# A planned one-core attention and feed-forward kernel: products take tiles by their own gates, GpSimd does three of the clears, and the order table is made anew

## The chip, the cores and the metric

The kernel runs on one core of one Trainium2 chip. The metric is the device time in microseconds (us) of one execution. Engines are named as in the profile: PE is TensorE, which multiplies; PEld is its weight load; DVE is VectorE, ACT is ScalarE, POOL is GpSimd and SP is SyncE. POOL, SP and ACT also issue DMA transfers.

## The reference

There are 8 batches of 8 heads, 576 positions and 64 values a head. Attention adds a bias that depends on the distance of two positions and on the head; its output is laid out as 4608 tokens of 512 values and goes through a feed-forward layer of 2048 with a periodic gate.

```python
scores = q @ k.T / 8 + bias_table[bucket(|i - j|)]      # 32 buckets, one value a head
attn   = exp(scores) / sum(exp(scores))
x      = (attn @ v) laid out as 4608 x 512
h      = x @ w_in                                        # 4608 x 2048
s      = sin(alpha * h)
g      = h + s * s / alpha
out    = g @ w_out                                       # 4608 x 512, float32
```

## The kernel before

**Attention.** A batch is called t, a pair of heads p. K and Q are needed with the head's 64 values on the partitions. For the first two batches (and Q of the third) POOL loads natural tiles into xT, and PE turns them by transposes (L1089; the very first pair in halves, L1069, out of two loads that SP and ACT issue and that DVE and ACT cast, L931 and L933). For later batches POOL stages 16-bit copies in device memory (L990), and SP's queue loads them turned (L996). Scores are products of 64 rows at a time (L1148), with the last 64 positions apart (L1109, L1114, L1138). ACT takes the exponential of 1024 columns at once into a tile u (L1155); DVE multiplies the part near the diagonal by the exponential of the bias (L1176, L1160, L1163). PE multiplies by V (L1190, L1199), DVE divides (L1209, L1210), and the result is turned into xT, by PE for batch 0 (L1223) and by SP's queue after that (L1216).

**Feed-forward.** The tokens go in nine blocks of 480 to 576. For each block there are 16 units, one for each 128 of the 2048 columns. In a unit PE makes four products of 512 columns (L1242), ACT takes the sine (L1249), DVE squares it (L1253) and makes the gate g (L1267), which also sets the unit's accumulator free. An output tile is 128 tokens; it needs 16 products with w_out (L1276), one for each unit's gate, which the kernel emits as eight pieces of two. DVE then copies the tile out (L1282) and SP stores it (L1285). Accumulators lie in eight banks; units use banks 0 to 5, and a score tile takes a pair of banks.

**Order.** `_graph` makes a list of tasks with an engine, a cost and the tasks that each depends on, and `_Plan.run` plays them through in time: each engine takes the next task as soon as its dependencies, its buffers and its banks allow. If the table LINE is given, each engine takes its tasks in that table's order (a text of differences between task numbers), and the play-through settles what remains: how the engines' streams interleave in the program and which bank each product gets. The engines then execute in exactly that order; a task that waits holds up all that stands behind it on its engine.

**Where the change touches.** In `moe_out` a tile's first piece waits for all 16 gates of its blocks (`deps += G_done[b]`), each tile waits for the last piece of the tile before it (`state["mo"]`), and `held` keeps a first unit of the next block ahead of the fourth tile. `memsets` (L951 to L960, DVE) clears five kinds of tile before the first casts. POOL's first transfer (L963) stands first in its queue. The planner's cost of `memsets`, of the first loads and of POOL's first transfer stand in `_graph`.

Of the kernel before, what the change touches and what calls it, by code (L numbers as in the profile page):

```python
# [406 lines left out]
def _graph(K, opt):  # L407
    plan = _Plan()
# [4 lines left out]
    add = plan.add  # L413
# [16 lines left out]
    for half in range(2):  # L430
        for kind in range(2):
            first[kind][half] = add("ACT" if kind else "SP", 0.45, E("first_load", kind, half),
                                    lat=3.6 - 0.4 * kind if half else 2.95, prio=-9 + 0.3 * half)
# [4 lines left out]
    t_ms = add("DVE", 2.4, E("memsets"), prio=-10)  # L438
# [11 lines left out]
    def gq(dur, f, args, deps=(), pipe=1.0, pkt=58):  # L450
        return add("POOL", dur, E(f, *args), deps=deps, pipe=pipe, seq="GQ", pkt=pkt)

    def load_nat(t, p):
        for kind in range(2):
            if (t, p) != (0, 0) and (t < 2 or kind in nat2):
                T_nat[t][p][kind] = gq(0.67 if plan.nseq.get("GQ") else 1.3, "load_nat",
                                       (t, p, kind), pipe=0.78, pkt=90)
# [257 lines left out]
    BLK = _blocks(opt["blk"])  # L715
# [40 lines left out]
    def moe_out(tau):  # L756
# [4 lines left out]
        early = bs[-1] == len(BLK) - 1 and opt["early_mo"]  # L761
        np_ = opt["mo_n"]
        fn = NF // np_
        for piece in range(np_):
            fs = range(fn * piece, fn * piece + fn)
            deps = [T_wout[fs[-1] // 4]]
            for b in bs:
                deps += [G_done[b][f] for f in fs]
                if not piece and not early:
                    deps += G_done[b]  # L770
            if last is not None:
                deps.append(last)
            elif tau:
                deps.append(state["mo"])
            m = add("PE", 0.2158 * fn, None, deps=deps, prio=opt["p_mo"] - 0.01 * (piece > 0),
                    take=[(1, users)] if piece == 0 else [], mode="full", name=f"mo{tau}")
            if piece == 0:
                j = tau - state["tau0"]
                if bs[-1] + 1 < NBLK - 1 and j in opt["hold"]:
                    held.setdefault((bs[-1] + 1, opt["hold"][j]), []).append(m)  # L780
                m.emit = lambda m=m, fs=fs: K.moe_out(cell, tag(m), tau, fs)
            else:
                m.emit = lambda fs=fs: K.moe_out(cell, None, tau, fs)
            last = m
# [49 lines left out]
    0}, early_mo=False, mo_n=8, ins={-1: {16: 16}, 0: {}, 1: {5: 16}, 2: {15: 16}, 7: {15: 12,  # L834
# [8 lines left out]
class _Ops:  # L843
# [105 lines left out]
    def memsets(self):  # L949
        nc = self.nc  # L950
        nc.vector.memset(self.blank, 0.0)  # L951
        for i in range(2):
# [6 lines left out]
            nc.vector.memset(self.kd[i], 0.0)  # L959
            nc.vector.memset(self.us[i], 0.0)  # L960
# [377 lines left out]
```

## Time and profile before

| | us |
|---|---|
| median of three runs | 391.63 |
| lowest and highest | 390.82, 392.54 |
| the profiled execution | 391.27 |
| its span, first to last instruction | 389.4 |

The span is 1.87 us shorter than the profiled execution's time. In the rows quoted below, a line of the timeline has the start, the length, the engine, the source line, the operation, what it writes and reads, the shape and the count of instructions; in brackets stands the idle time of the engine before it and what ended that. Matmul lengths include a tail in the pipeline, so a group of back-to-back matmuls ends later than the next one starts. The table of stages gives for each engine the busy us in a stretch, then the clock that TensorE was granted as a share of full speed.

### The profile page before, as it was taken

The numbers are of one execution on the slowest core, as the hardware profiler recorded it, in microseconds if no ns is written. First come the engines' busy times: TensorE is split into PE (matmuls) and PEld (weight loads), VectorE is DVE, ScalarE is ACT, GpSimd is POOL, SyncE is SP. The second block draws the span as 40 slices with busy tenths as digits, with TensorE's granted clock in tenths as the row PEclk, the third lists the DMA queues.
The fourth block names the chain that finished last, engine by engine and source line by source line (L and its number), as shares of the span: only waits on it lengthen the run. The fifth ranks groups of instructions, "written<-read, shape, count | busy, mean of one in ns | idle before, by whom it ended". The sixth has DMA issues, their size and how long they took to land.

```text
span 389.4 us, 9321 instructions
## 1 busy us (share of the span) xinstructions
PE 372.6 (96%) x3811; PEld 202.0 (52%) x3811; DVE 297.2 (76%) x738; ACT 279.6 (72%) x339; POOL 85.8 (22%) x101
## 2 busy tenths in 40 slices
PE   2989979999999999999999999999999999999996
PEld 1567435665446545564555545544654445444442
DVE  5588897769967798759966986799649879978422
ACT  2799878899799868996799689958986874343100
POOL 7685734081006200900090004000000000000000
PEclk9999998999999999999999999999999999999999
DMA  9999999999739994999299839600420020201014
GB/s 162 184 186 187 195 182 145 158 116 184 85 77 138 138 61 106 109 179 150 39 153 150 117 64 171 89 14 0 117 62 0 29 72 28 72 0 56 0 56 162
DMA packets 148170, 40.79 MB, mean 105 GB/s; under 512 B 134416, under 2 KB 143456, under 8 KB 148128
## 3 DMA queue, kind: packets, MB, share of 16 engines
q0 software_dynamic: 96656, 18.45, 62.3%
q1 hardware_dynamic: 50768, 21.22, 26.6%
q8 instruction: 30, 0.49, 0.5%
q10 hardware_dynamic: 704, 0.53, 0.5%
q14 instruction: 12, 0.10, 0.1%
HBM read 36.94 MB, written 15.93 MB: 136 GB/s over the span
## 4 chain that ended last, share of the span: by engine, by line
PE 85%; DMA 11%; POOL 2%; DVE 1%; issue 0%; ACTq 0%; ACT 0%; SPq 0%; POOLq 0%
PE acc L1276 33%; PE acc L1242 28%; PE acc L1199 9%; PE acc L1148 8%; DMA xT<-in_q_dram 4%; DMA w_in<-in_moe_w_in_dram 2%; PE acc L1190 2%; PE acc L1109 2%; DMA v<-in_v_dram 2%; DMA cst_sb<-cst 2%; PE acc L1138 1%; DMA toep<-e_sb 1%; POOL xT L963 1%; PE acc L1089 0%; POOL mt L1042 0%
## 5 line engine op out<-in xcount | busy, mean ns | idle before, releaser
L1155 ACT ACTIVATE u<-acc 128x1024 f16<-128x1024 f32 x160 | 154.6, 1026 | 19.4 <-PE acc L1148 15.3
L1276 PE MATMUL acc<-w_out,g 128*128 128x512 f16 x576 | 145.9, 381 | 0.0
L1249 ACT ACTIVATE s<-acc,alphaT 128x512 f16<-128x512 f32 (+2 forms) x144 | 96.1, 688 | 58.0 <-PE acc L1242 32.5
L1242 PE MATMUL acc<-xT,w_in 128*128 128x512 f16 (+2 forms) x640 | 134.9, 358 | 0.0
L1267 DVE SCALAR_TENSOR_TENSOR g<-s,inv_a,acc 128x512 f16<-128x512 f16 (+4 forms) x176 | 107.5, 646 | 1.5
L1242 PEld LDWEIGHTS <-w_in 128*128 128x128 f16 x640 | 59.0, 98 | 67.0 <-issue 0.7
L1276 PEld LDWEIGHTS <-g 128*128 128x128 f16 x576 | 50.8, 98 | 53.9 <-issue 8.1
L1253 DVE TENSOR_TENSOR s<-s 128x512 f16<-128x512 f16 (+2 forms) x144 | 57.2, 420 | 16.8 <-ACT s L1249 16.5
L1176 DVE TENSOR_TENSOR u<-u,toep 128x1024 f16<-128x1024 f16 (+1 forms) x128 | 58.9, 486 | 14.3 <-ACT u L1155 13.8
L969 POOL DMA_DIRECT2D v<-in_v_dram x32 | 28.3, 897 | 144.8 <-PE acc L1199 136.5
L1199 PE MATMUL acc<-v,u 128*128 128x65 f16 x1280 | 53.9, 193 | 0.0
L1199 PEld LDWEIGHTS <-u 128*128 128x128 f16 x1280 | 49.9, 97 | 4.2
L1148 PE MATMUL acc<-qT,kT 64*128 64x256 f16 x512 | 45.0, 282 | 3.6 <-DVE g L1267 1.9
L1282 DVE COPY outs<-acc 128x512 f32<-128x512 f32 x36 | 24.6, 688 | 20.4 <-PE acc L1276 18.8
L1148 PEld LDWEIGHTS <-kT 64*128 64x128 f16 x512 | 19.5, 96 | 26.7 <-issue 23.6
L1210 DVE TENSOR_TENSOR xp<-acc,rden 128x256 f16<-128x256 f32 (+1 forms) x64 | 31.4, 491 | 2.2
L1190 PE MATMUL acc<-vt,u 128*128 128x130 f16 x128 | 28.3, 221 | 0.3 <-DMA vt<-in_v_dram 0.3
L1209 DVE RECIPROCAL rden<-acc 128x4 f32<-128x4 f32 (+1 forms) x64 | 11.9, 185 | 20.3 <-PE acc L1199 20.2
L1190 PEld LDWEIGHTS <-u 128*128 128x128 f16 x128 | 12.4, 97 | 8.0 <-issue 2.9
L990 POOL DMA_DIRECT2D staged_q<-in_q_dram x5 | 13.9, 2780 | 0.0
L990 POOL DMA_DIRECT2D staged_k<-in_k_dram x6 | 13.5, 2257 | 0.9 <-DMA xT<-in_q_dram 0.9
L1249 ACT ACT_TABLE_LOAD x9 | 11.5, 1283 | 0.2
(62 smaller groups left out, 163.6 us busy)
## 6 DMA issues: line engine op xcount, KB each, us to landing
out_dram<-outs SPq DMA_DIRECT2D x36, 256.0 KB, 2.4
v<-in_v_dram POOLq DMA_DIRECT2D x32, 128.0 KB, 7.3
staged_k<-in_k_dram POOLq DMA_DIRECT2D x6, 576.0 KB, 13.0
staged_q<-in_q_dram POOLq DMA_DIRECT2D x5, 576.0 KB, 15.4
w_in<-in_moe_w_in_dram POOLq DMA_DIRECT2D x4, 512.0 KB, 8.6
w_out<-in_moe_w_out_dram POOLq DMA_DIRECT2D x4, 512.0 KB, 10.1
xT<-in_q_dram POOLq DMA_DIRECT2D x11, 144.0 KB, 7.8
xT<-in_k_dram POOLq DMA_DIRECT2D x7, 144.0 KB, 6.9
```

Of the source, the lines that this page charges most:

```text
L969: self.nc.gpsimd.dma_start(out=self.vs[t % 2][:, c, :, 0:D], in_=src)
L1148: self.nc.tensor.matmul(out=s[:, o:o + 256], lhsT=self.kT[t % 2][r, p, 128 * c:128 * c + 128], rhs=self.qT[t % 2][r, p, 256 * w:256 * w + ...
L1155: self.nc.scalar.activation(out=c["u"], in_=c["s"], func=AF.Exp, scale=0.125)
L1176: self.nc.vector.tensor_tensor(out=io, in0=io, in1=m, op=ALU.mult)
L1190: nc.tensor.matmul(out=c["av"][:, 130 * j:130 * j + 130], lhsT=tail, rhs=vt[:, p, :], start=True, stop=True, skip_group_check=True)
L1199: nc.tensor.matmul(out=c["av"][:, 130 * j + 65 * a:130 * j + 65 * a + 65], lhsT=l, rhs=vv[:, ch, 2 * p + a, 0:65], start=False, stop=True, ...
L1210: self.nc.vector.tensor_tensor(out=self.ap(x, 256 * w, [[64, n], [1, 64]]), in0=self.ap(av, 0, [[65, n], [1, 64]]), in1=self.ap(r, 0, [[1, ...
L1242: self.nc.tensor.matmul(out=c["h"][:, x:y], lhsT=self.w_in[:, j, 128 * f:128 * f + 128], rhs=self.xT[:, j, lo + x:lo + y], start=(j == 0), ...
L1249: self.nc.scalar.activation(out=c["s"], in_=c["h"], func=AF.Sin, scale=self.alphaT[:, f:f + 1])
L1253: self.nc.vector.tensor_tensor(out=c["s"], in0=c["s"], in1=c["s"], op=ALU.mult)
L1267: self.nc.vector.scalar_tensor_tensor(out=o, in0=c["s"][:, x:y], scalar=self.inv_a[:, f:f + 1], in1=c["h"][:, x:y], op0=ALU.mult, op1=ALU.add)
L1276: self.nc.tensor.matmul(out=c["mo"], lhsT=self.g[b][:, f, 128 * (tau % 4):128 * (tau % 4) + 128], rhs=self.w_out[:, f, :], start=(f == 0), ...
```

## The change

1. `moe_out`: the option `early_mo` is gone, and a new option `strict`, which is False, switches off three things: the first piece's wait for all gates of its blocks, the wait for the tile before, and the hold against the next block's first unit. A piece now depends on its own two gates, its weights and the piece before it in its own tile.
2. Clears: `blank`, the two `kd` and the two `us` tiles are no longer cleared by DVE. A new task `clear` has POOL do it, ahead of POOL's first transfer. Per partition these are 2 x 320, 2 x 512 and 256 values of 16 bits, 1920 in all, in five instructions.
3. Costs in `_graph`: 1.5 for the DVE clears (2.4 before), 1.0 for the new ones, 0.9 for the first transfer of POOL (1.3 before), and changed latencies of the first loads.
4. LINE is replaced by another table, so that the order on every engine is another.

```diff
-                                    lat=3.6 - 0.4 * kind if half else 2.95, prio=-9 + 0.3 * half)
+                                    lat=3.4 - 0.1 * kind if half else 2.95 - 0.25 * kind, prio=-9 + 0.3 * half)
...
-    t_ms = add("DVE", 2.4, E("memsets"), prio=-10)
+    t_ms = add("DVE", 1.5, E("memsets"), prio=-10)
+    add("POOL", 1.0, E("clear"), seq="GQ")
...
-                T_nat[t][p][kind] = gq(0.67 if plan.nseq.get("GQ") else 1.3, "load_nat",
+                T_nat[t][p][kind] = gq(0.67 if plan.nseq.get("GQ") > 1 else 0.9, "load_nat",
...
-        early = bs[-1] == len(BLK) - 1 and opt["early_mo"]
...
-                if not piece and not early:
+                if not piece and opt["strict"]:
                     deps += G_done[b]
             if last is not None:
                 deps.append(last)
-            elif tau:
+            elif tau and opt["strict"]:
                 deps.append(state["mo"])
...
-                if bs[-1] + 1 < NBLK - 1 and j in opt["hold"]:
+                if opt["strict"] and bs[-1] + 1 < NBLK - 1 and j in opt["hold"]:
...
     def memsets(self):
         nc = self.nc
-        nc.vector.memset(self.blank, 0.0)
         for i in range(2):
...
-            nc.vector.memset(self.kd[i], 0.0)
-            nc.vector.memset(self.us[i], 0.0)
+
+    def clear(self):
+        nc = self.nc
+        for i in range(2):
+            nc.gpsimd.memset(self.us[i], 0.0)
+            nc.gpsimd.memset(self.kd[i], 0.0)
+        nc.gpsimd.memset(self.blank, 0.0)
```

What the new table does to the order on PE around block 0, in names of the tasks (a piece is two products with w_out; "1 of tile 0" is its first piece):

```text
before: units 0.0 0.1, V product, units 0.2 to 0.15, turns of (2,1) and (2,0), score a, score b,
        turn, two scores, turn, score, pieces 1 2 of tile 0, scores, piece 3 of tile 0, ...
after:  units 0.0 0.1, V product, units 0.2 to 0.6, piece 1 of tile 1, unit 0.7, piece 1 of tile 0,
        units 0.8 to 0.12, piece 2 of tile 0, unit 0.13, piece 2 of tile 1, units 0.14 0.15,
        piece 3 of tile 1, score a, piece 4 of tile 1, piece 3 of tile 0, piece 5 of tile 1,
        pieces 4 5 of tile 0, two scores, piece 6 of tile 1, turn of (2,3), score b,
        pieces 7 8 of tile 1, scores, piece 6 of tile 0, V product of (1,0), ...
```

At the start, PE's order was: half turns of K and Q, with a whole turn of pair 1 second in the queue, the bias and the other halves between, then the first scores. Now it is three half turns (K, Q, K), the bias product, the first scores, the last half turn, and only then the turns of pair 1. DVE casts both halves of K before Q's.

More of the change, by code (lines that the diff above doesn't have):

```diff
@@ L833 @@
     line=_line(LINE), c_act=((1, 1),), h_act=(), p_bias=-0.5, nu=12, ng=3, first=(1, 1, 1), bs=2, win=7, hold={3:
-    0}, early_mo=False, mo_n=8, ins={-1: {16: 16}, 0: {}, 1: {5: 16}, 2: {15: 16}, 7: {15: 12,
+    0}, strict=False, mo_n=8, ins={-1: {16: 16}, 0: {}, 1: {5: 16}, 2: {15: 16}, 7: {15: 12,
     16: 4}, 5: {17: 16}, 4: {18: 16}}, s_at={0: 9, 1: 9}, blk=(512, 512, 512, 512, 512, 512,
```

100 rows, old and new, of the table LINE are left out of this document.

## The prediction

> **What bounds the kernel now.** First the page's busy times and slices, then the stages, then PE's waits.
>
> ```profile
> span 389.4 us, 9321 instructions
> PE 372.6 (96%) x3811; PEld 202.0 (52%) x3811; DVE 297.2 (76%) x738; ACT 279.6 (72%) x339; POOL 85.8 (22%) x101
> PE   2989979999999999999999999999999999999996
> ...
> DVE  5588897769967798759966986799649879978422
> ```
>
> PE is busy for 372.6 of 389.4 us and hardly stops between slice 7 and the end. The products are the same ones after the change, so a gain can only come from the 16.8 us in which PE stands idle, from stretches where it runs slowly, or from less switching of its array. The stages say where these are:
>
> ```profile
> core 0: us, PE busy (x) PEld busy (x) DVE busy (x) ACT busy (x) POOL busy (x), PEclk, DMA share, GB/s
> 0.00:22.00 22.00, 13.18 (x191) 9.00 (x191) 12.72 (x39) 11.80 (x15) 16.41 (x31) 1.00 1.23 174
> 22.00:39.40 17.40, 16.08 (x376) 12.71 (x368) 14.66 (x45) 16.66 (x21) 12.38 (x19) 1.00 1.47 185
> 39.40:55.00 15.60, 14.90 (x86) 6.69 (x82) 14.49 (x33) 12.58 (x18) 8.76 (x11) 1.00 1.56 193
> 55.00:63.50 8.50, 6.28 (x93) 3.25 (x93) 7.65 (x16) 7.08 (x10) 6.21 (x5) 0.80 1.67 150
> 63.50:90.00 26.50, 26.50 (x427) 17.15 (x426) 17.86 (x56) 23.57 (x26) 9.52 (x9) 1.00 1.70 141
> 130.00:389.00 259.00, 255.67 (x2236) 131.80 (x2232) 196.91 (x473) 173.44 (x213) 23.25 (x22) 1.00 0.66 80
> ```
>
> Up to 39.4 us lies the set-up with batch 0; from 22 us on ACT leads there (16.66 of 17.40). Then come block 0's units. The stage from 55 to 63.5 is the odd one: PE idles for 2.2 us and its granted clock is 0.80, the only one below 1.00. After that PE is full; 3.3 us idle remain in the last 259, most of them the final copy and store. What happens at 55 us:
>
> ```profile
> 54.49 0.69 ACT L1249 ACTIVATE s<-acc,alphaT 128x512 f16<-128x512 f32 x1 [0.43 <-DVE g L1267]
> 57.31 2.06 DVE L1267 SCALAR_TENSOR_TENSOR g<-s,inv_a,acc 128x512 f16<-128x512 f16 x3
> 42.18 12.38 PE L1242 MATMUL acc<-xT,w_in 128*128 128x512 f16 x56
> 55.07 0.70 PE L1089 MATMUL acc<-ident,xT 96*64 96x96 f16 x24 [0.51 <-DMA xT<-in_q_dram]
> 55.78 0.40 PE L1148 MATMUL acc<-qT,kT 64*128 64x256 f16 x4
> 58.10 0.39 PE L1148 MATMUL acc<-qT,kT 64*128 64x256 f16 x4 [1.93 <-DVE g L1267]
> 58.71 0.63 PE L1089 MATMUL acc<-ident,xT 96*64 96x96 f16 x12 [0.21 <-DMA xT<-in_q_dram]
> ```
>
> PE ends block 0's units at 54.56, but DVE makes their gates until 59.37, 4.8 us behind. Two turns wait 0.51 and 0.21 for Q of batch 2, and a score product waits 1.93 for a bank that a late gate still holds.
>
> **The change part by part.** Sums are made against the profiled execution's 391.27 (span 389.4), which lies 0.36 below the median of 391.63.
>
> *The stall at 56 us.* In the new order ten pieces stand ahead of that second score product: four inside block 0's units, one behind them, five between the two scores. A piece of two products costs 0.43:
>
> ```profile
> 72.94 0.86 PE acc L1276 x4
> 71.80 0.54 PE acc L1276 x2
> ```
>
> Four products take 0.86. The five pieces between the scores are 2.16 us, more than the 1.93 of the wait. The other five fill 2.16 while DVE catches up, whose gates end no later than before. The turns of batch 2 move behind them, past 59.5 us, when their transfers have landed. Their 0.51 and 0.21 go as well. **-1.93 and -0.72.**
>
> *The clock behind the stall.* Compare equal work:
>
> ```profile
> 60.16 0.69 PE L1089 MATMUL acc<-ident,xT 96*64 96x96 f16 x12
> 61.32 1.47 PE L1276 MATMUL acc<-w_out,g 128*128 128x512 f16 x4
> 65.47 0.82 PE L1276 MATMUL acc<-w_out,g 128*128 128x512 f16 x3
> 35.10 0.45 PE L1089 MATMUL acc<-ident,xT 96*64 96x96 f16 x12
> ```
>
> Twelve transposes take 0.69 against 0.45, four products 1.47 where three take 0.82. A clock of 0.80 over 8.5 us is 1.7 us lost. If the stall goes, no other PE idle time after 40 us is longer than 0.5, so I take the whole: **-1.70**. Bounds: 0 (the dip has another cause) and -1.7. [...]
>
> *Switching.* A group of two products followed by scores takes 0.54 (above), 0.11 more than its half of 0.86, for the change of array shape. Counted in the two programs, neighbours of different shape are 190 before and 187 after: **-0.30**.
>
> *What is late next.* Work that moves forward is missing later. When PE comes to the second V product of batch 1 (at 63.94 before), it has issued 14 pieces instead of 3, and three turns fewer. Of the stage from 63.5 to 90, where PE had 26.50 us of work, 11 x 0.432 = 4.75 leave and 3 x 0.45 = 1.35 come: 23.1. ACT has 23.57 there, and the copy of one turn (0.5) moves in: 24.1. So ACT takes over as the bound of this stage and PE waits for exponentials: **+1.0**. Bounds: 0 (later units move up) and +2.0 (ACT doesn't get its scores at the right times).
>
> *The clears.* They give DVE nothing, as it waits for its first load anyway, and they hold back POOL's transfers:
>
> ```profile
> 3.41 0.19 DVE L960 MEMSET us<- 128x160 uint32 x1
> 5.11 1.71 DVE L933 CAST xT<-toep 96x384 f16<-96x384 f32 x3 [1.50 <-DMA toep<-in_q_dram]
> 0.83 0.17 DVE L951 MEMSET blank<- 128x128 uint32 x1 [0.83 <-PEq L1322]
> 1.86 0.27 DVE L959 MEMSET kd<- 128x256 uint32 x1
> 1.29 0.77 POOL L963 DMA_DIRECT2D xT<-in_k_dram  x1 [0.84 <-POOLq L1322]
> 18.25 0.34 POOL L1042 COPY mt<-toep 64x192 f16<-64x192 f16 x1 [1.02 <-DMA toep<-e_sb]
> 7.43 0.69 PE L1089 MATMUL acc<-ident,xT 96*64 96x96 f16 x12 [0.74 <-DMA xT<-in_k_dram]
> 10.61 1.04 PE L1148 MATMUL acc<-qT,kT 64*128 64x256 f16 x8
> 41.57 0.23 PE L1190 MATMUL acc<-vt,u 128*128 128x130 f16 x1 [0.26 <-DMA vt<-in_v_dram]
> ```
>
> On DVE the five take 0.17 + 2 x (0.27 + 0.19) = 1.1 us: the lower bound on POOL. POOL's copy of 192 values took 0.34, so 1920 values would be 3.4: the upper. The first transfer starts at 1.29 and ends a wait at 7.43. After the change its turn stands behind the first scores. These went out at 10.61 before; if they go out 1 us sooner, the turn comes at 9.6, and 2.2 us of delay are covered. Later transfers queue behind each other (DMA share over 1 throughout), so V of batch 1, which ends a wait of 0.26 at 41.57, comes late by at most what of the delay is not covered. The set-up's own order lets scores start earlier, but PE must still take V at about 41.5 before unit 0.2. So what is gained ahead of it is mostly waited for. Bounds: -1.1 (the 1.32 us that PE idles from 22 to 39.4, less the part that the wait for V keeps) and +1.2 (3.4 less 2.2 covered). Nearest to the row at 41.57, which already shows PE waiting for that queue: **+0.30**.
>
> Sum: -1.93 - 0.72 - 1.70 - 0.30 + 1.00 + 0.30 = -3.35; 391.27 - 3.35 = **387.9 us**.
>
> **The rivals.**
>
> *The clock comes late at the start (slower).* At the start too PE runs slowly:
>
> ```profile
> 18.03 1.03 PE L1148 MATMUL acc<-qT,kT 64*128 64x256 f16 x8
> 34.56 0.61 PE L1148 MATMUL acc<-qT,kT 64*128 64x256 f16 x8
> 29.70 0.45 PE L1089 MATMUL acc<-ident,xT 96*64 96x96 f16 x12
> ```
>
> Eight score products take 1.03 at 18 us and 0.61 at 34.6, although the granted clock reads 1.00 in both stages; by 29.7 transposes are fast. The speed came after a stretch from 15.6 to 21 with hardly a gap. The new order puts scores earlier, so PE waits for ACT's exponentials more often in this very stretch. If no stretch is long enough, slow running goes on. Slow work takes about 0.55 more (0.69 against 0.45, 1.03 against 0.61), and the 16.08 us of work up to 39.4 have 1.32 of slack: slow to 39.4 costs 8.8 - 1.3 = 7.5, giving 395.4. It ends above 393.2, that is slower by over 0.5%, once about 12 us of this work run slowly, a release at about 35 us instead of near 21. For it: the order has more waits there. Against it: ACT and PE were both near full from 22 on, and a queue of transposes stands between the scores.
>
> *Pieces wait for their own gates (no change).* The free products now stand closer behind their gates. With rows' lengths the nearest piece stood 6.5 us behind its unit before and 2.6 after; eight of 288 stand nearer than 5.1. Gates ran 4.8 us late at the end of block 0. If they do so everywhere, the shortfalls add up to some 5 us; half of it is 2.5, and the time 390.4. A piece that waits holds all PE work behind it. Against it: DVE is 76% busy over the run, and the two nearest pieces stand in the last block, behind 330 us, where DVE's slices fall to 8 and then 4.
>
> *The dip has another cause (no change).* If the clock falls at this place for a reason other than the idle time, such as a time since the start, it falls again: 387.9 + 1.7 = 389.6. [...] Against it: 0.80 in just the stage with the longest stall, 1.00 in all others.
>
> **How the numbers follow.** Chances: forecast 0.70, late clock 0.12, pieces that wait 0.11, dip that stays 0.07. A measurement can tell about 0.5% (1.96 us) from no change: against 391.27, faster is below 389.3 and slower above 393.2. The forecast's bounds: -1.1 instead of +0.3 and 0 instead of +1.0 give 385.5 at the best, seldom both; at the worst 2.0 and 1.2 give 389.8. To 386.0 below, and above as far as the pieces that wait, 391.0. Faster 0.70, same 0.18, slower 0.12, the late clock alone being slower.
>
> **What would show it.** Right: no PE wait over 1 us between 40 and 65, a clock of 1.00 in every stage, ACT at over 95% between 62 and 86 with short PE waits for u there, and V of batch 1 ending a wait at 41 to 42.5. Wrong: scores of 1 us for eight behind 25 us; PE waits at L1280 (L1276 before) for g; a clock under 1.00 near 56 to 63; or a first transfer of POOL so late that the turns of pair 1 hold back the scores.

## The result and the profile after

The changed kernel takes **388.6 us** (median of 7, 388.0 to 390.15) and the kernel before 391.32 beside it (median of 7, 390.58 to 393.52). The ratio is 0.9929, with an interval of 0.9902 to 0.9955: faster by 0.7%. The forecast was 387.9, with a range from 386.0 to 391.0. The profiled execution took 388.6, 2.67 less than the one of before.

The page of the changed kernel, its busy times and slices:

```profile
span 386.8 us, 9311 instructions
...
PE 373.5 (97%) x3811; PEld 203.5 (53%) x3811; DVE 299.5 (77%) x733; ACT 279.5 (72%) x339; POOL 88.5 (23%) x106
...
PE   4989999999999999999999999999999999999996
...
DVE  4489797779995797769965996789756959899634
```

PE is busy 0.9 us longer in a span that is 2.6 shorter; its idle time fell from 16.8 to 13.3. The stages of the changed kernel, and the one stage of before that was not shown:

```profile
core 0: us, PE busy (x) PEld busy (x) DVE busy (x) ACT busy (x) POOL busy (x), PEclk, DMA share, GB/s
0.00:22.00 22.00, 14.62 (x203) 9.50 (x204) 10.99 (x28) 12.39 (x15) 18.20 (x34) 1.00 1.24 176
22.00:39.40 17.40, 16.04 (x331) 12.99 (x330) 14.97 (x48) 14.45 (x17) 13.06 (x19) 1.00 1.43 178
39.40:55.00 15.60, 15.60 (x111) 7.70 (x111) 13.47 (x32) 13.15 (x19) 9.42 (x11) 1.00 1.58 193
55.00:63.50 8.50, 8.50 (x80) 3.63 (x77) 7.92 (x16) 7.48 (x10) 6.08 (x5) 1.00 1.65 164
63.50:90.00 26.50, 26.29 (x458) 17.62 (x455) 20.29 (x57) 24.05 (x28) 7.81 (x8) 1.00 1.55 152
90.00:130.00 40.00, 39.41 (x412) 20.68 (x410) 33.29 (x79) 33.47 (x41) 10.64 (x9) 1.00 1.13 122
```

```profile
90.00:130.00 40.00, 40.00 (x429) 21.36 (x427) 32.92 (x82) 34.48 (x42) 9.23 (x8) 1.00 1.11 123
```

From 55 to 63.5 PE is full at a clock of 1.00, where it stood at 6.28 of 8.50 and 0.80. New are 0.21 of idle time from 63.5 to 90 and 0.59 from 90 to 130, where before had none. PE around block 0's end, after the change:

```profile
56.79 0.59 PE L1280 MATMUL acc<-w_out,g 128*128 128x512 f16 x2
57.31 0.39 PE L1152 MATMUL acc<-qT,kT 64*128 64x256 f16 x4
57.64 2.33 PE L1280 MATMUL acc<-w_out,g 128*128 128x512 f16 x10
59.90 0.61 PE L1152 MATMUL acc<-qT,kT 64*128 64x256 f16 x8
```

The five pieces (ten products, L1280) stand between the two scores and fill 2.33 us, and the second score needs no wait. No row has a bracket.

**Where the time went.** Up to two points PE has made exactly the same products in both kernels, and at a third the difference is known, so the times at these points can be compared as they are. They are read from the 3811 matmul rows of each trace:

```
PE starts                           products ahead   before   after   after - before
its first product                      0                6.24    3.86    -2.38
block 0's first unit                 559 in both       39.41   40.64    +1.23
its third unit                       585 in both       42.18   42.97    +0.79
block 1's first unit                1161 and 1177      90.11   90.12    +0.01
its last product                    3810 in both      385.29  382.68    -2.61
```

At block 1's first unit the changed kernel has made 16 products with w_out more and is otherwise as far. At the forecast's price of 0.432 for two these are 3.46 us of work. So three stretches can be set beside the forecast, whose switching term of -0.30 has no place of its own:

```
us                    measured                   forecast
up to 42              +0.79                      +0.30
from 42 to 90         0.01 - 0.79 - 3.46 = -4.24 -4.35 + 1.00 = -3.35
from 90 to the end    -2.62 + 3.46 = +0.84       0
together              -2.61                      -3.35 with switching
```

The stages give the middle stretch in another way: from 39.4 to 90 idle time falls from 2.92 to 0.21, and the clock of 0.80 over 8.5 us, 1.70 lost, is gone; together 4.41. The gain stands where it was forecast, and it is larger there by 0.9, since the loss of 1.00 that was forecast behind it didn't come. More than forecast was lost at two other places, in the set-up and behind 90 us.

**The clock in many executions.** The runs also list the mean granted clock of each execution. In the 107 executions of the kernel before that were taken beside the experiments, 10 had a mean clock of 0.997 or more and took 389.26 on average; 54 had 0.993 to 0.997 and took 390.78; 43 had less and took 392.16. The profiled one, with 0.80 over 8.5 us, belongs to the middle group. All 19 executions of the changed kernel (7 above, 12 below) had 0.998 or more and took 388.95 on average. So the executions in which the clock falls are what puts the average of all 107 (391.19) 1.9 us above that of the ten, and against these ten the changed kernel is only 0.3 ahead. Of the average gain of 2.24 us (391.19 to 388.95) nearly all goes with the clock. The ten are picked by their clock, and no trace shows one of them: whether PE waited as long in them isn't known.

### The profile page after: what moved, and what is told of

Its sections match the earlier page's. It is cut to its first block, busy times and chain, and to the rows that moved or that the text cites. A ratio compares the mean times of both kernels' runs of the same rounds, so it can differ in the third digit from the quotient of the medians.

```text
span 386.8 us, 9311 instructions
## 1 busy us (share of the span) xinstructions
PE 373.5 (97%) x3811; PEld 203.5 (53%) x3811; DVE 299.5 (77%) x733; ACT 279.5 (72%) x339; POOL 88.5 (23%) x106
## 4 chain that ended last, share of the span: by engine, by line
PE 90%; DVE 4%; ACT 3%; DMA 1%; issue 1%; ACTq 0%
PE acc L1280 33%; PE acc L1246 31%; PE acc L1152 9%; PE acc L1203 9%; ACT u L1159 3%; PE acc L1194 2%; PE acc L1113 2%; PE acc L1142 1%; PE acc L1093 1%; DMA cst_sb<-cst 1%; DVE xp L1214 1%; DVE u L1180 1%; DVE kd L1007 1%; PE acc L1118 1%; DVE outs L1286 0%
## 5 line engine op out<-in xcount | busy, mean ns | idle before, releaser
L1280 PE MATMUL acc<-w_out,g 128*128 128x512 f16 x576 | 146.2, 380 | 0.0
L1271 DVE SCALAR_TENSOR_TENSOR g<-s,inv_a,acc 128x512 f16<-128x512 f16 (+4 forms) x176 | 106.3, 643 | 1.6
L1280 PEld LDWEIGHTS <-g 128*128 128x128 f16 x576 | 50.5, 98 | 53.7 <-issue 7.8
L1180 DVE TENSOR_TENSOR u<-u,toep 128x256 f16<-128x256 f16 (+1 forms) x128 | 58.9, 486 | 16.1 <-ACT u L1159 15.8
L1203 PE MATMUL acc<-v,u 128*128 128x65 f16 x1280 | 55.6, 195 | 0.0
L1203 PEld LDWEIGHTS <-u 128*128 128x128 f16 x1280 | 51.4, 99 | 5.1 <-issue 0.2
L1194 PEld LDWEIGHTS <-u 128*128 128x128 f16 x128 | 12.6, 98 | 7.6 <-issue 2.5
```

Of the source, the lines that this page charges most:

```text
L1180: self.nc.vector.tensor_tensor(out=io, in0=io, in1=m, op=ALU.mult)
L1194: nc.tensor.matmul(out=c["av"][:, 130 * j:130 * j + 130], lhsT=tail, rhs=vt[:, p, :], start=True, stop=True, skip_group_check=True)
L1203: nc.tensor.matmul(out=c["av"][:, 130 * j + 65 * a:130 * j + 65 * a + 65], lhsT=l, rhs=vv[:, ch, 2 * p + a, 0:65], start=False, stop=True, ...
L1271: self.nc.vector.scalar_tensor_tensor(out=o, in0=c["s"][:, x:y], scalar=self.inv_a[:, f:f + 1], in1=c["h"][:, x:y], op0=ALU.mult, op1=ALU.add)
L1280: self.nc.tensor.matmul(out=c["mo"], lhsT=self.g[b][:, f, 128 * (tau % 4):128 * (tau % 4) + 128], rhs=self.w_out[:, f, :], start=(f == 0), ...
```

## The experiments

The theory of the forecast: PE's idle time at block 0's end costs twice, as a wait and as a slower clock behind it, and pieces that fill it gain both; the clears cost little. Its rivals: the dip has another cause; the clock at the start decides; and, since the set-up and the stretch behind 90 us gave back 1.6, the question of what does that.

### One part undone, or one part done alone

**The clears back on DVE**, in the changed kernel:

```diff
     def clear(self):
...
-        for i in range(2):
-            nc.gpsimd.memset(self.us[i], 0.0)
-            nc.gpsimd.memset(self.kd[i], 0.0)
-        nc.gpsimd.memset(self.blank, 0.0)
...
     def memsets(self):
+        nc.vector.memset(self.blank, 0.0)
...
+            nc.vector.memset(self.kd[i], 0.0)
+            nc.vector.memset(self.us[i], 0.0)
```

> The changed kernel with the five clears back on DVE, all else as in the changed kernel. If the gain comes from the products that fill the stall at 56 us, the time stays near the changed kernel's 388.6 us, within 0.8, and the stage from 55 to 63.5 keeps a clock of 1.00. If the clears carry the gain (the rival: POOL's later transfers leave the first loads more room), the time goes back towards 391.3 us. In both cases POOL's first transfer should start near 1.3 us instead of 2.5, and the first loads should land up to 0.9 us later.

Measured: 390.06 (388.63 to 391.95, 12 executions), ratio 0.9978 (0.9955 to 1.0). That is neither number: 1.5 above 388.6 and 1.2 below 391.3. All twelve kept a mean clock of 0.998 or more. The profiled execution was the quickest, 388.63, with the clock at 1.00 from 55 to 63.5 and a wait of 1.5 for the constants (0.8 in the changed kernel), so no trace shows what made the others slower. **The clears on POOL alone**, in the kernel before, with the five DVE clears taken out:

```diff
     def load_nat(self, t, p, kind):
+        if not self.cleared:
+            self.cleared = True
+            for i in range(2):
+                self.nc.gpsimd.memset(self.us[i], 0.0)
+                self.nc.gpsimd.memset(self.kd[i], 0.0)
+            self.nc.gpsimd.memset(self.blank, 0.0)
```

> The kernel before with the five clears moved to POOL ahead of its first transfer, and nothing else. By the theory of the filled stall: 391.3 us within 0.8, with the wait of 1.9 us for the late gate and the low clock behind it unchanged. By the rival that the clears bring the gain: about 389 us.

Measured: 391.69 (390.52 to 395.81, 12), ratio 1.0026 (1.0 to 1.0053), as the stall theory has it: in the old order the clears gain nothing. POOL in the changed kernel:

```profile
0.74 0.36 POOL L962 MEMSET us<- 128x320 f16 x1 [0.29 <-POOLq L1326]
1.04 0.53 POOL L963 MEMSET kd<- 128x512 f16 x1
...
2.28 0.31 POOL L964 MEMSET blank<- 128x256 f16 x1
2.54 0.77 POOL L967 DMA_DIRECT2D xT<-in_k_dram  x1
```

The five clears move POOL's first transfer from 1.29 to 2.54: a delay of 1.25, at the lower of the forecast's ends (1.1 and 3.4). In the old order PE's waits then show it (the view has what is waited for, then us in total, times and the longest):

```profile
PE acc L1093 <- DMA xT<-in_k_dram: 3.8, 3, 1.8
```

In that kernel's profiled execution PE waits 3.8 us for K, against 0.9 in the kernel before. In the new order, where turns of pair 1 stand behind the first scores, PE waits for none of POOL's transfers of K and Q. So the forecast's cover is right there: the 1.25 us cost nothing that the profile shows. Whether the clears on POOL even gain in the new order is open, and with it whether they carry a part of the change's gain. The medians say 1.0 to 1.5 gained, but the two intervals meet, and the same exchange in another pair of kernels below went 0.85 the other way.

**All ten pieces behind the stall.** The changed kernel with the order of ten tasks altered (`_move` takes the listed tasks out of the table and puts them behind the last one named):

```diff
+OPT["line"] = _move(OPT["line"], (284, 274, 275, 285, 286, 287, 276, 288, 277, 278), 331)
```

> The changed kernel with the ten pieces of block 0's output tiles moved behind the two scores that follow the units, as they stood before the change; everything else as changed. If the ten pieces fill the stall and so keep the clock, the stall of about 2 us and a granted clock of about 0.8 in the stage from 55 to 63.5 come back: 3.6 us lost there, up to 1.3 us given back in the stages from 63.5 to 130, where PE has more to fill in; about 391 us. If the gain lies in the set-up or in the freer order later on, the time stays at 388.6.

Measured: 395.67 (394.78 to 396.43, 6), ratio 1.0121 (1.0091 to 1.0151), 4.7 above the number of the stall theory. **Only the five between the two scores** moved behind the same place, with the other five left inside the units:

```diff
+OPT["line"] = _move(OPT["line"], (287, 276, 288, 277, 278), 331)
```

> The changed kernel with only the five pieces that stand between the two scores at 58 us moved behind unit 0's late work (behind the same item as in the run where ten were moved, which took 395.67). If the price of the stall is the wait plus the fall of the clock behind it, a wait of about 2 us at L1161 comes back and a clock near 0.80 from 55 to 63.5, and the pieces give back at most 1 us later: 391.0 to 392.5. If a shorter wait leaves the clock alone: 390 to 390.7 at a clock of 1.00. If what cost so much with ten pieces is their new place and not the stall: half of the 7 us, 392 with no wait over 1 us at 58.

Measured: 391.96 (391.05 to 393.14, 12), ratio 1.0035 (1.0015 to 1.0054). PE with ten pieces moved, and then with five:

```profile
57.75 0.40 PE L1161 MATMUL acc<-qT,kT 64*128 64x256 f16 x4 [0.96 <-DVE g L1280]
59.94 0.37 PE L1161 MATMUL acc<-qT,kT 64*128 64x256 f16 x1 [1.79 <-DVE g L1280]
60.60 1.01 PE L1161 MATMUL acc<-qT,kT 64*128 64x256 f16 x7 [0.29 <-DVE g L1280]
...
61.89 4.45 PE L1289 MATMUL acc<-w_out,g 128*128 128x512 f16 x10
```

```profile
59.35 0.27 PE L1161 MATMUL acc<-qT,kT 64*128 64x256 f16 x1 [1.47 <-DVE g L1280]
60.01 0.66 PE L1161 MATMUL acc<-qT,kT 64*128 64x256 f16 x7 [0.39 <-DVE g L1280]
...
60.84 3.55 PE L1289 MATMUL acc<-w_out,g 128*128 128x512 f16 x9
```

The wait for the late gate (g) comes back in both, and behind it the pieces run slowly in these executions: ten products in 4.45 and nine in 3.55, where ten took 2.33. Their stages:

```profile
55.00:63.50 8.50, 5.45 (x33) 2.23 (x31) 7.23 (x15) 6.71 (x9) 5.17 (x4) 0.78 1.74 162
63.50:90.00 26.50, 26.29 (x367) 15.29 (x365) 15.69 (x44) 17.43 (x20) 0.00 (x0) 0.94 0.99 109
```

```profile
55.00:63.50 8.50, 6.64 (x40) 2.77 (x39) 6.64 (x14) 6.58 (x8) 5.33 (x4) 0.87 1.75 161
63.50:90.00 26.50, 26.29 (x425) 16.36 (x422) 18.27 (x52) 21.23 (x24) 3.81 (x5) 0.98 1.23 130
```

With ten, PE idles 3.05 of the 8.50 us, and the clocks of 0.78 and 0.94 cost 0.22 x 8.50 + 0.06 x 26.50 = 3.5 more; the median rose by 7.1. With five, it idles 1.86 and the clocks cost 0.13 x 8.50 + 0.02 x 26.50 = 1.6; the median rose by 3.4, into the range of the theory of wait and clock. But only seven of the twelve executions with five lost the clock. The other five kept a mean clock of 1.0 and still took 391.61 on average, 2.7 above the changed kernel, and the seven 392.37. So the clock is worth 0.8 there and not half of the price; the wait of 1.86, if it was as long in those, is most of the rest, and some 0.8 stays open. With ten the stall and the slow stretch (0.78 and then 0.94) are longer than the ones of before, and the up to 1.3 that were to be given back later were not: the stage from 90 to 130 still has 0.58 of idle time, as in the changed kernel. That was the first sign that what is late there is not the work that moved forward.

**The stall kept and filled with unused products**, in the kernel before: 18 products of a cleared tile that nothing reads, ahead of the score that waits.

```diff
     def qk_t(self, s, t, p, w, half):
+        if (t, p, w, half) == (1, 1, 0, 1):
+            for _ in range(18):
+                self.fill("full", 7)
```

> The kernel before with 18 products of 256 columns of a cleared tile, which nothing reads, ahead of the score that waits for the late gate. The wait itself stays (no useful work is moved), but PE isn't idle in it. If idle time makes the clock fall, the granted clock stays at 1.00 in the stage from 55 to 63.5 and the time falls by about 1.7 us, to 389.6. If the dip has another cause (a time since the start), it stays at 0.80 and the time at 391.3 or a little over.

Measured: 389.84 (387.99 to 390.44, 12), ratio 0.9962 (0.9939 to 0.9984).

```profile
56.08 0.40 PE L1151 MATMUL acc<-qT,kT 64*128 64x256 f16 x4 [0.59 <-DVE g L1270]
56.40 2.14 PE L1060 MATMUL acc<-blank 128*128 128x256 f16 x18
58.48 0.39 PE L1151 MATMUL acc<-qT,kT 64*128 64x256 f16 x4
```

```profile
55.00:63.50 8.50, 7.91 (x138) 5.15 (x133) 8.35 (x17) 8.43 (x11) 5.04 (x3) 1.00 1.80 161
```

The score goes out at 58.48, no sooner than before (58.10): the wait is as long, but PE is kept busy in it. The clock stays at 1.00, and eleven of the twelve executions had a mean clock of 0.998 or more. The time falls by 1.4 (391.22 to 389.84). So the idle time is what lowers the clock here, and the clock alone is worth 1.4; the rival "another cause" falls. In the kernel before, a gap of 1.93 us, with 0.51 us idle shortly ahead of it and 0.21 behind it, was followed by a granted clock of 0.50 from 58.81 to 62.21.

### The slow start

In the changed kernel PE runs at half speed longer than before (twelve transposes take 0.69 at 16.72 and 0.45 at 38.38; 0.69 is also what they take in the kernel before at 60.16, at a granted clock of 0.50):

```profile
25.34 1.03 PE L1152 MATMUL acc<-qT,kT 64*128 64x256 f16 x8
...
27.48 0.65 PE L1203 MATMUL acc<-v,u 128*128 128x65 f16 x8
...
28.49 0.40 PE L1203 MATMUL acc<-v,u 128*128 128x65 f16 x8
```

and in the kernel before:

```profile
22.57 0.41 PE L1199 MATMUL acc<-v,u 128*128 128x65 f16 x8
```

Eight scores take 1.03 until 25 us and eight V products 0.65 at 27.5; full speed (0.40) comes at about 28, where before it was there at 22.5. The granted clock reads 1.00 in both kernels' first stages: the column doesn't show half speed there.

**Unused products ahead of the first turn**, in the changed kernel, with `blank` cleared first on DVE:

```diff
     def turn_half(self, cell, bank, kind, half):
+        if not kind and not half:
+            for _ in range(14):
+                self.fill("full", 0)
```

> The changed kernel with 14 unused products of a cleared tile put on PE ahead of the first turn, where PE waits for its first load (first matmul at 3.86 us); the tile is cleared on DVE. Theory A (running at half speed until about 28 us costs time in the set-up): eight scores fall from 1.04 to about 0.61 before 20 us, the PE time lost up to 39.4 us falls by 1 to 2, and the time is 386.6 to 387.6. Theory B (ACT bounds the set-up, so slow products hide beside it): scores are fast early, but PE waits for u grow by as much, and the time stays at 388.6 within 0.5. Theory C (products this early don't release the clock, or it falls again in the waits that follow): eight scores still take 1.03 at 20 us, time 388.6 or up to 0.5 more.

Measured: 388.97 (388.19 to 389.52, 9), ratio 0.9951 (0.9931 to 0.997). **The same, and unused products in the waits that the planner foresees up to 30 us**, by one option:

```diff
-    act1=((1, 0), (1, 1), (2, 0), (3, 0)), fill=0, nat2=(1,), early=('X0.0', 'T0.0', 'X0.1',
+    act1=((1, 0), (1, 1), (2, 0), (3, 0)), fill=30, nat2=(1,), early=('X0.0', 'T0.0', 'X0.1',
```

> As the run with 14 unused products at the start, and unused products also in the waits of PE that the planner foresees up to 30 us. Theory A: the clock is held once it is released, eight scores take 0.61 from 10 us on, time 386.0 to 387.5. Theory B: no gain, 388.6, or up to 2 us more where an unused product stands ahead of a score that is already there. Theory C: speed comes at about 15 us by unbroken work, in between: 387.5 to 388.6.

Measured: 388.86 (386.55 to 390.95, 12), ratio 0.9943 (0.9918 to 0.9968); the profiled execution was the quickest of the twelve, 386.55. The time is theory B's. PE with the start alone:

```profile
1.06 3.17 PE L1064 MATMUL acc<-blank 128*128 128x256 f16 x14 [1.06 <-DVE blank L951]
...
7.03 0.61 PE L1155 MATMUL acc<-qT,kT 64*128 64x256 f16 x8
...
8.88 1.17 PE L1096 MATMUL acc<-ident,xT 96*64 96x96 f16 x24 [0.79 <-DMA xT<-in_q_dram]
...
10.52 0.69 PE L1096 MATMUL acc<-ident,xT 96*64 96x96 f16 x12
...
19.25 1.03 PE L1155 MATMUL acc<-qT,kT 64*128 64x256 f16 x8
```

Behind 3.17 us of products eight scores are fast (0.61 at 7.03, against 1.04 at 7.42 in the changed kernel), but three waits of 0.79 to 0.88 follow between 4.6 and 8.9, and from the row at 8.88 on speed is gone again (24 transposes in 1.17, against 0.70 in the next run): theory C. With the waits filled, speed holds (0.61 at 7.3, at 14.85 and 21.3), and that execution's span is 2.0 shorter (384.8 against 386.8); but over twelve executions the median is no better. The next run shows one thing that is late then. **The same with the clears on DVE:**

```diff
     def clear(self):
-        for i in range(2):
-            nc.gpsimd.memset(self.us[i], 0.0)
-            nc.gpsimd.memset(self.kd[i], 0.0)
...
     def memsets(self):
...
+            nc.vector.memset(self.kd[i], 0.0)
+            nc.vector.memset(self.us[i], 0.0)
```

> The changed kernel with 14 unused products at the start and unused products in the foreseen waits up to 30 us (388.86 median), and with the five clears back on DVE, so that POOL's first transfer starts about 1.25 us earlier. Theory A: with PE at full speed the set-up is bound by POOL's transfers (waits of 0.52 to 0.79 for Q and K at 10, 16 and 31 us in that run), and these shrink by up to 1.25 us together: 387.5 to 388.3. Theory B: the transfers wait for one another and not for POOL's start, the waits stay: 388.9 within 0.5. Theory C: DVE, with 1.1 us more at the start, holds back the first turns as it did the constants' wait in the run with only the clears moved (390.06): 389.5 to 390.5.

Measured: 388.01 (386.84 to 390.71, 12), ratio 0.993 (0.9904 to 0.9956); profiled 387.59. The median lies in theory A's range, but the intervals of this run and the last overlap widely. PE's waits for K and Q fell from 1.9 to 1.3 in all, and two others came:

```profile
38.44 1.90 PE L1248 MATMUL acc<-xT,w_in 128*128 128x512 f16 x8
41.35 0.23 PE L1196 MATMUL acc<-vt,u 128*128 128x130 f16 x1 [1.01 <-DMA vt<-in_v_dram]
```

PE now comes to the first V product of batch 1 at 40.3 and waits there 1.01 for V. In the changed kernel it came at 42.38 and waited for nothing:

```profile
42.38 0.22 PE L1194 MATMUL acc<-vt,u 128*128 128x130 f16 x1
```

Here V's arrival takes back a part of what PE gained ahead of it, as the forecast argued. In the quickest execution with `fill=30` it doesn't: PE is busy for 15.57 of the 15.60 us from 39.4 to 55, and the profile lists no wait for V. The other wait is 0.9 for the constants. **Four more unused products ahead of each K turn of batch 1**, where the run with `fill=30` had its longest idle time behind the start (0.79 ahead of the turn at 31.23):

```diff
     def turn(self, cell, bank, t, p, kind):
         cell[kind] = bank
+        if t == 1 and not kind:
+            for _ in range(4):
+                self.fill("full", bank)
```

> The same kernel of 388.86 with four more unused products ahead of each K turn of batch 1 (0.43 us each at full speed), where its longest idle time (0.96 us at 30.2) stood. Its executions ran from 386.55 to 390.95, those above 390 at a mean granted clock of 0.991 or less. Theory A: the clock falls in these executions because of that idle time: the spread narrows and the median comes to 387.0 to 388.2. Theory B: the clock falls elsewhere, or the time follows the arrival of transfers: median 388.9 within 0.6, up to 1 us more for 1.3 us of added products, and the same spread.

Measured: 388.81 (387.83 to 391.61, 12), ratio 0.9955 (0.9928 to 0.9981): theory B, the spread is nearly as wide. **The kernel before with all these fills:**

```diff
     def turn_half(self, cell, bank, kind, half):
+        if not kind and not half:
+            for _ in range(14):
+                self.fill("full", 0)
...
     def qk_t(self, s, t, p, w, half):
+        if (t, p, w, half) == (1, 1, 0, 1):
+            for _ in range(18):
+                self.fill("full", 7)
```

(and `fill=30` for `fill=0`)

> The kernel before with the 18 unused products ahead of the late score (389.84 alone), 14 unused products at the start and unused products in the foreseen waits up to 30 us. Theory A: what the change gains is the idle time at block 0's end and the clock, and both can be had without its order: 388.3 to 389.3, as the changed kernel so filled (388.86). Theory B: the new order is worth something of its own (transfers waited for no longer, less switching, about 1 us): 389.5 to 390.3, and the changed kernel so filled stays ahead by 0.7 or more.

Measured: 391.50 (390.25 to 393.61, 12), ratio 1.0019 (0.9997 to 1.0041). Neither theory's number: it is 1.7 worse than with the 18 products alone. The clock isn't the reason, since eight of the twelve kept a mean clock of 0.999 or more and took 391.31 on average. In its trace full speed comes only at 17 us, behind twelve unused products of 2.02 us (eighteen take 2.14 at 56.68), and PE still waits 0.93 for ACT's exponential at 21.3. Theory A falls: the old order can't be filled to the changed kernel's time in this way. How much of the difference is the order and how much the places of the fills isn't told apart.

**V one unit later**, on top of the best of these (fills, clears on DVE):

```diff
+OPT["line"] = _move(OPT["line"], (197,), 218)
```

> The changed kernel with unused products up to 30 us and the clears on DVE (388.01), and the first V product of batch 1 moved behind one more product group of block 0 (0.86 to 0.95 us), where PE waited 1.01 us for the transfer of V at 40.3. Theory A (that transfer bounds the set-up once PE runs at full speed): the wait falls below 0.2, time 387.0 to 387.7. Theory B (what comes later is bound by another, DVE's gates or ACT's exponentials of batch 1): the wait goes, and as much comes back before 130 us; 388.0 within 0.5.

Measured: 388.38 (386.7 to 391.54, 12), ratio 0.9925 (0.9894 to 0.9955); the profiled one took 389.3. The wait for V is gone, as theory A has it, but the median isn't lower than without the move: neither theory's range covers the spread. Its profiled execution shows where speed was lost this time:

```profile
8.60 0.35 PE L1021 MATMUL acc<-tab,cst_sb 32*128 32x8 f32 x2 [2.03 <-DMA cst_sb<-cst]
...
11.25 0.69 PE L1104 MATMUL acc<-ident,xT 96*64 96x96 f16 x12
```

PE waits 2.03 for the constants, where the run with only the clears on DVE and fills waited 0.9; behind these 2.03 us of idle time PE is at half speed from about 11 (0.69 for twelve transposes at 11.25, against 0.45 at 5.36). **The changed kernel itself again, beside it** (no edit):

> The changed kernel itself once more, so that it is compared with the run beside it on the same chip: 388.6 within 0.6, no execution at a mean granted clock below 0.998, eight scores at 1.03 until 25 us. If the runs with unused products are better than it by chance alone, the two medians of this call agree within 0.5; if filling is worth 0.6 and the later V product 0.5 to 1.0, they differ by 0.8 to 1.6.

Measured: 389.09 (387.89 to 389.64, 12), ratio 0.9944 (0.992 to 0.9968). So 0.7 lies between these two, which were measured side by side, between the two numbers that were expected, and the intervals overlap: nothing here is shown to beat the changed kernel. By the mean clock the filled versions look better when they keep it, and they lose it often: executions at 0.997 or more took 387.7 (7 of 12, clears on DVE), 387.6 (7 of 12, V later), 387.9 (6 of 12, clears on POOL) and 388.6 (9 of 12, with four more at the turns), against 388.95 for 19 of 19 of the changed kernel. The others took 389.5 to 389.9, and 391.4 with four more at the turns. As these are picked by their clock, it is a sign and not a test.

## Why the prediction was right, and where it was not

1. **The stall, -1.93 and -0.72: right.** The pieces cover it (2.33 us between the scores), no wait over 1 us is left between 40 and 65, and moving the five back brings a wait of 1.47 + 0.39.
2. **The clock, -1.70: right in mechanism; the size was that of the one execution in the profile.** Shown from both sides: idle time brought back lowers it (0.78 with ten, and 0.87 with five, where seven of twelve executions lost it), the same wait filled keeps it (1.00, -1.4 us). Over the executions of the kernel before, the groups by clock lie 0, 1.5 and 2.9 us above the ten that kept it; the profiled one stood in the middle. It is the largest part of the gain. Apart from it, little is left on the average: 0.3, where the profiled pair has -2.61 + 1.70 = -0.9.
3. **Switching, -0.30:** not tried by itself. The traces have the 190 and 187 pairs of neighbours that were counted, but three pairs can't be told from the rest of the sum.
4. **What is late next, +1.00: the wrong place and cause; that a loss of nearly this size came all the same is luck.** ACT was to take over between 63.5 and 90, busy over 95% from 62 to 86. It has the work that was forecast (24.05, forecast 24.1), and it doesn't bind: from 62 to 86 it is busy 21.70 of 24.00, and PE waits for it once, 0.2. What came is +0.84 behind 90 us, and the largest single wait there is at 95 us. The timeline that leads to it:

```profile
88.60 3.11 DVE L1007 COPY kd<-kT 64x256 f16<-64x256 f16 x2
...
88.61 2.81 POOL L994 DMA_DIRECT2D staged_q<-in_q_dram  x1
...
95.17 0.75 DVE L1271 SCALAR_TENSOR_TENSOR g<-s,inv_a,acc 128x512 f16<-128x512 f16 x1
...
95.97 1.02 PE L1246 MATMUL acc<-xT,w_in 128*128 128x512 f16 x4 [0.51 <-DVE g L1271]
```

Two small copies of DVE take 3.11 us together. One of them lasted 2.87, and it ended 0.05 after POOL had finished issuing a staged transfer (88.61 + 2.81 = 91.42). In the kernel before these copies took 0.45 together, at 92.1, when POOL had long issued its transfers:

```profile
86.08 2.80 POOL L990 DMA_DIRECT2D staged_q<-in_q_dram  x1
...
92.10 0.45 DVE L1003 COPY kd<-kT 64x256 f16<-64x256 f16 x2
...
93.97 0.75 DVE L1267 SCALAR_TENSOR_TENSOR g<-s,inv_a,acc 128x512 f16<-128x512 f16 x1
```

DVE then comes late to block 1's gates, the first at 95.17 instead of 93.97, and PE, which in the new order makes six units' products in a row from 90.12, has to wait for a bank. It is no accident of one execution: in all seven profiles of kernels with the new table in which these copies were read, one of the twelve took 2.77 to 2.87, and the twelve average 0.44; in the three with the old table none is over 0.23, and they average 0.22. In the three of the seven that were read beside POOL's rows, the copies start 0.01 to 0.02 ahead of the staged issue. Not every issue of POOL does it. Later in the same run two such copies take 0.49 together beside the issue of V's transfers:

```profile
247.56 0.49 DVE L1007 COPY kd<-kT 64x256 f16<-64x256 f16 x2
247.74 1.28 POOL L979 DMA_DIRECT2D vt<-in_v_dram  x2
```

So that the copy waits for POOL is a reading of the rows, and why it would wait is not shown. No run moved the copy away from the issue, so what the 0.84 us would be without it stays open; the one wait is 0.51 of it.

5. **The set-up, +0.30: the size was off (+0.79), and the reason another one.** The clears delay POOL's transfers by 1.25, which the new order covers. What costs is what the rival named: half speed until about 28 instead of 22.5. PE starts its first product 2.38 sooner and is still 1.23 later at block 0's first unit; with the waits filled, the clears on DVE and full speed early it gets there at 38.44 instead of 40.64. Eight scores at 1.03 behind 25 us were one of the forecast's signs of being wrong, and they came. They did not decide, because full speed came at about 28 and not at the 35 us from which it would have. V hides a part: at the third unit 0.79 of the 1.23 is left, and the run with fills and clears on DVE, which is 2.2 sooner at the first unit and then waits for V, has a span only 1.0 shorter than the changed kernel's (385.8 against 386.8).

The rival "pieces wait for their own gates" did not show: PE has no wait at L1280 at all. The sum held because the large terms stood on rows that showed the loss itself. That the rest came out near was partly luck: a loss that was forecast from ACT didn't come, and one that nobody forecast, behind 90 us, took its place.

## What to carry to other kernels

Before one counts what a wait costs, one should look at what runs behind it: here a wait of 1.93 us was followed by 3.4 us at a clock of 0.50 (0.80 over 8.5 us), and independent products put into the wait gained both. One should also look at many executions: the profiled one had the clock's usual loss, and others had none or twice as much. A forecast of "who is late next" needs the engines' queues at the new times, not busy sums: ACT had just the sum that was forecast and still wasn't the one. And a short copy should be looked at again where it is moved to: here one of DVE took 2.77 to 2.87 us instead of 0.22 in all seven profiles with the new order that were read for it, and in three of these it is seen beside a transfer issue of POOL of 2.8 us.

## What the runs showed of the hardware

- In the kernel before, a PE wait of 1.93 us was followed by a granted clock of 0.50 for 3.4 us (0.80 over the 8.5 us of the stage). Slow products also followed waits of 1.47 and 0.39 with a product between (nine in 3.55) and of 0.96, 1.79 and 0.29 (ten in 4.45, against 2.33 in the changed kernel). With 18 unused products (2.14 us) put into the wait of before the clock read 1.00. Behind 3.17 us of products at the start eight scores took 0.61 at 7.03; with waits of 0.88, 0.81 and 0.79 among short work, twelve transposes took 0.69 again at 10.52.
- The same program keeps its clock in some executions and not in others: of before's 107, 10 kept it, and those took 389.26 on average against 391.19 for all. Of the twelve of the changed kernel with five pieces moved back, 5 kept it.
- In the changed kernel the granted clock reads 1.00 in the first two stages while eight scores take 1.03 at 19.14 and 25.34, against 0.61 at 38.75.
- POOL clears 320, 512 and 256 16-bit values a partition in 0.36, 0.53 and 0.31 us; five of these moved its first transfer by 1.25.
- A DVE copy of 256 values a partition took 2.87 us beside a 2.81 us issue of a staged transfer by POOL, against a median of 0.22 for the twelve of its kind, and 0.22 and 0.25 beside the issues of V's transfers.
